# New orders of the matmuls within a head, and the value projection's buffers moved in SBUF

## The chip, the cores and the metric

The kernel runs on one core of a Trainium2 chip. A core has a matrix engine, TensorE (PE in the profile; PEld is its loading of weights), and engines that work beside it: VectorE (DVE), ScalarE (ACT), GpSimd (POOL) and SyncE (SP, used here to issue DMAs). PE writes to PSUM, which has eight banks of 512 fp32 columns; DVE and ACT read from there. The metric is the device time of one execution in microseconds (us), the median of several runs.

## What is computed

Two attentions over the same input x (2048 rows of 576 numbers, 32 heads of 18 numbers each), mixed by a gate:

```python
g = _sigmoid((x * gate_w).sum(-1, keepdims=True))
a = _A_ref(x, A_wqkv, A_wo)      # 32 heads, keys and values of their own
b = _B_ref(x, B_wq, B_wk, B_wv, B_wo)   # 32 heads, one key and value for all
return g * a + (1 - g) * b
```

Each head is `softmax(q @ k.T / sqrt(18)) @ v`. So 64 heads of 2048 x 2048 scores are computed, their exponentials taken, multiplied by the values and normalised, and the two results go through output matrices and are added. The kernel takes the exact maximum of each row of scores before the exponentials.

## The kernel before

**Stages.** First the projections of queries and keys (to DRAM, in two fp16 parts, a high and a low one), then the projection of the values together with the first maxima (T below 0 in the code), then the main stage, and a short last one. Heads u = 0 to 31 are those of B (one key tile, `ksb`), 32 to 63 those of A.

**The main stage** is one loop over T, the tiles of 128 keys: 16 tiles a head, two per step, so eight steps ("rows") a head. Three things run at once at different distances:

- Maxima of the head that comes LEAD = 22 tiles later. A matmul (L537) makes 128 x 512 scores in a bank, DVE takes the maximum of each row (L553). In the strings of the order such a matmul is `m`. `N` is an `m` whose bank and that of the one before are read by one DVE instruction of 1024 columns (L551), when the two banks are neighbours. `x` makes the difference of two key blocks and ACT takes its positive part (L540, tile xb); `c` is the block to which DVE then adds xb while it takes the maximum (L543). So x and c save one reading.
- Scores and exponentials, `s`: a matmul (L598), which ACT reads and exponentiates into one of 16 slots of the tile pt (L587). `S` is an `s` that is read together with the one before in one ACT instruction of 1024 columns, when the two banks are neighbours.
- The product with the values, two tiles later, `p0` and `p1` (L613, four matmuls that fill the columns of the array side by side, each in two passes over fp32): `p0f` is a full tile of 512 columns, `p0h` a half, 256 columns, and a second `h` finishes it. The sums stay in bank 7.

Queries and keys lie twice in SBUF, in rows 0 to 55 for scores and 64 to 117 for maxima, so that a matmul of either kind uses its own half of the array's rows, and two can run side by side.

**Banks.** Scores and x take the least recently used of banks 0 to 3, maxima, c and the output units that of banks 4 to 6. The order of use starts anew with each head.

**The order within a row** is written out by hand as strings, one string a row and eight a head. PE runs them as they stand. There are four sets: PLAIN for heads without output units, ONE for heads with one unit, TWO for two, EACH for the last heads with a unit in every row. A unit `U` is 12 matmuls of the output projection (L742), whose sum goes out by ACT (first part) or DVE (second part). Heads 33 to 52 have units: ONE for 33, 36, 38, 41, 43, 46, 48 and 51, TWO for the other twelve. PLAIN holds for 0 to 32 (but for the first row of head 0, FIRST) and 53 to 58 (but for the last row of 58), EACH from there. `steps_pair` (L920) reads a string and places the operations.

At the end of a head DVE copies bank 7 to the tile oe (L635), in the first row of the next head.

**The value projection's buffers.** `project_v` (L315) writes 32 blocks through three tiles `vst`, by ACT (L321) and then a DMA to v_d, issued from ACT's queue. They are the last tiles of the pool `stp`, on the right side of SBUF. The pools of the first stages (xpool, wpool, stp, later vwp) are laid from the right end inwards; when they are closed (`open_ph2`, L493), pt and others are laid on the left side behind what is there, and the key tiles ksa and others from the right end. Where a new tile lies over an old one, its first write waits for the last use of the old one.

Of the kernel before, what the change touches and what calls it, by code (L numbers as in the profile page):

```python
# [8 lines left out]
F32 = mybir.dt.float32  # L9
# [10 lines left out]
S = 2048  # L20
# [29 lines left out]
def gated_mix_kernel(ctx: ExitStack, tc: tile.TileContext, xT, wall, wv, wo, out):  # L50
    nc = tc.nc
    P = 128
# [80 lines left out]


    ph1 = ExitStack()
    xpool = ph1.enter_context(tc.tile_pool(name="xpool", bufs=1, side="right"))
    wpool = ph1.enter_context(tc.tile_pool(name="wpool", bufs=2, side="right"))
    stp = ph1.enter_context(tc.tile_pool(name="stp", bufs=3, side="right"))
# [169 lines left out]
        nc.vector.tensor_copy(vb[:, 4 * c:4 * c + 4, 0:18],  # L308
                              pv[:, 0:72].rearrange("p (j d) -> p j d", d=18))

    vst = [stp.tile([P, 16, 19], F32, name=f"vst{i}", bufs=1) for i in range(3)]
    for t in vst:
        nc.gpsimd.memset(t, 1.0)

# [550 lines left out]
    def due(T, t0, t1, n):  # L865
        if t0 == SEG[0][3]:
# [6 lines left out]


    FIRST = "s m s c s m s m s m s m s m s x"
    PLAIN = ("c s x s m m S p0h s m s m p0h m s S m s p1f",
# [7 lines left out]
    ONE = ("s m s m p0f m s m s m s p1f s x c s m s U",  # L884
# [7 lines left out]
    TWO = ("p0h s c S m m s p0h p1h m s s m p1h s x s m s m U",  # L892
# [7 lines left out]
    EACH = ("p0f m s s m m s p1f m s s x s c U m s m s",  # L900
# [8 lines left out]
    def pair_order(T):  # L909
        n = len(UNITS.get(T // 16, ()))  # L910
        return (EACH if T >= SEG[1][3] else TWO if n == 2 else ONE if n else PLAIN)[T % 16 // 2]

# [53 lines left out]
    for T in range(-LEAD, NSTEP + 2, 2):  # L966
# [15 lines left out]
        for op in order.split():  # L982
            k, second, c = op[0], op[1:2] == "B", op[2:]
# [86 lines left out]
```

## Time and profile before

| | us |
|---|---|
| Median of 3 runs | 2667.53 (2667.22 to 2669.83) |
| The profiled execution | 2669.34 |
| Its span, first to last instruction | 2667.6 |
| Mean granted clock of PE | 0.996 |
| Projections, up to the first score | 0 to 276.2 |
| Main stage, first to last copy of a finished head | 321.65 to 2610.6 |

The profile is one execution. A row of a timeline has the start, the length, the engine, the line in the code, the operation, the tile written and the tiles read; several instructions of one kind are merged, with their count. What stands in brackets is the idle time before, and what ended it. The length of an instruction on PE, DVE or ACT has a tail in which the next one already runs, so the time that each one costs in a full queue is read from start to start. A windows row has the length of a stretch, the busy time and count of PE, PEld, DVE, ACT and POOL, PE's granted clock (1.00 is full), the share of the DMA engines and GB/s.

### The profile page before, as it was taken

How to read it: one execution, taken by the hardware profiler on the slowest of the kernel's cores; microseconds unless marked ns; L12 is line 12 of the kernel's file. 1: busy time of each engine (PE TensorE's matmuls, PEld its weight loads, DVE VectorE, ACT ScalarE, POOL GpSimd, SP SyncE). 2: the span in 40 equal slices, each digit the busy share in tenths (PEclk: the TensorE clock that was granted, in tenths of full speed). 3: DMA queues.
4: the chain of work that ended last, by engine and by line, in shares of the span. 5: the costliest groups of instructions: out<-in, count | busy, mean ns of one | idle time of the engine just before them, and what ended most of it. 6: DMA issues, size and time to landing. Idle time of an engine off the chain costs nothing.

```text
span 2667.6 us, 59192 instructions
## 1 busy us (share of the span) xinstructions
PE 2643.6 (99%) x22798; PEld 946.5 (35%) x22798; DVE 2406.6 (90%) x4341; ACT 2388.4 (90%) x4334; POOL 284.0 (11%) x526
## 2 busy tenths in 40 slices
PE   9999999999999999999999999999999999999998
PEld 7788322222222222222222323332323332223444
DVE  8447899999999999999999999999999999998873
ACT  4331899999999999999999999999999999998785
POOL 4740000002001100100110001000100021001000
PEclk9999999999999999999999999999999999999999
DMA  6332000011001100110132113112211112123312
GB/s 202 122 114 77 23 20 19 19 31 48 25 20 46 44 19 19 51 36 17 39 77 83 42 47 91 59 34 60 77 52 51 46 59 65 40 60 96 90 36 95
DMA packets 127304, 150.18 MB, mean 56 GB/s; under 512 B 55456, under 2 KB 94744, under 8 KB 125933
## 3 DMA queue, kind: packets, MB, share of 16 engines
q1 hardware_dynamic: 112593, 119.38, 15.8%
q0 software_dynamic: 8096, 19.30, 2.1%
q10 hardware_dynamic: 6332, 7.71, 0.8%
q8 instruction: 179, 2.93, 0.4%
q14 instruction: 104, 0.85, 0.1%
HBM read 90.80 MB, written 46.45 MB: 51 GB/s over the span
## 4 chain that ended last, share of the span: by engine, by line
PE 89%; DVE 6%; ACT 3%; issue 1%; DMA 1%; POOL 0%; SPq 0%; ACTq 0%; DVEq 0%; POOLq 0%
PE bk L613 36%; PE bk L537 20%; PE bk L598 20%; PE bk L267 5%; PE bk L742 4%; DVE mx L553 3%; ACT pt L587 2%; PE bk L318 2%; DVE junk L543 1%; DVE mx L551 1%; DVE norm_a L209 0%; PE bk L807 0%; DVE pl L282 0%; SPq L56 0%; DVE oacc L815 0%
## 5 line engine op out<-in xcount | busy, mean ns | idle before, releaser
L587 ACT ACTIVATE pt<-bk 128x512 f32<-128x512 f32 (+1 forms) x3616 | 2091.4, 667 | 66.3 <-PE bk L598 41.5
L553 DVE TENSOR_REDUCE mx<-bk 128x1 f32<-128x512 f32 x2600 | 1624.5, 682 | 46.7 <-PE bk L537 27.1
L598 PE MATMUL bk<-qs,ksb 56*128 56x512 f16 x2688 | 798.4, 381 | 2.7 <-ACT pt L587 2.5
L537 PE MATMUL bk<-ksb,qs 54*128 54x512 f16 x2363 | 745.2, 381 | 3.5 <-DVE mx L553 1.6
L613 PE MATMUL bk<-pt,vb 128*19 128x256 f32 (+1 forms) x6656 | 593.3, 435 | 0.2 <-PE bk L537 0.2
L613 PE MATMUL bk<-pt,vg 128*19 128x256 f32 (+1 forms) x5504 | 555.1, 480 | 0.0
L537 PEld LDWEIGHTS <-qs 54*128 54x128 f16 x4096 | 290.0, 94 | 547.1 <-issue 478.9
L598 PE MATMUL bk<-qs,ksa 56*128 56x512 f16 x1408 | 404.9, 380 | 1.3 <-ACT pt L587 0.3
L537 PE MATMUL bk<-ksa,qs 54*128 54x512 f16 x1232 | 386.2, 379 | 2.9 <-DVE mx L553 2.2
L543 DVE CUSTOM_DVE_ANT_0 junk<-bk,xb 128x512 bf16<-128x512 f32 x501 | 343.6, 686 | 46.4 <-ACT pt L587 14.9
L598 PEld LDWEIGHTS <-ksb 56*128 56x128 f16 x2688 | 194.5, 94 | 367.2 <-issue 321.5
L540 ACT ACTIVATE xb<-bk 128x512 f32<-128x512 f32 x501 | 304.9, 609 | 5.5 <-PE bk L598 3.9
L551 DVE TENSOR_REDUCE mx<-bk 128x2 f32<-128x1024 f32 x247 | 300.4, 1216 | 1.1 <-PE bk L598 1.0
L613 PEld LDWEIGHTS bk<-pt,vb 128*19 128x19 f32 x6656 | 119.6, 97 | 269.1 <-issue 244.7
L563 POOL TENSOR_SCALAR mt<-mt 128x32 f32<-128x32 f32 x64 | 18.5, 290 | 1624.0 <-DVE mt L561 1624.0
L613 PEld LDWEIGHTS bk<-pt,vg 128*19 128x19 f32 x5504 | 96.8, 97 | 232.2 <-issue 223.8
L598 PEld LDWEIGHTS <-ksa 56*128 56x128 f16 x1408 | 97.1, 94 | 203.7 <-issue 181.5
L537 PE MATMUL bk<-kdb,qs 54*128 54x512 f16 x373 | 141.5, 379 | 0.0
L276 ACT ACTIVATE ph<-bk,tv 128x512 f16<-128x512 f32 x56 | 38.1, 686 | 97.6 <-PE bk L267 61.0
L282 DVE SCALAR_TENSOR_TENSOR pl<-bk,tv,ph 128x512 f16<-128x512 f32 x56 | 41.7, 748 | 71.3 <-ACT ph L276 41.2
L267 PE MATMUL bk<-xh,wh 128*128 128x512 f32 (+1 forms) x295 | 85.9, 389 | 0.8 <-ACT xh L360 0.7
L267 PE MATMUL bk<-xh,wl 128*128 128x512 f32 (+1 forms) x295 | 85.3, 387 | 0.0
(146 smaller groups left out, 1338.2 us busy)
## 6 DMA issues: line engine op xcount, KB each, us to landing
qs<-qkh SPq DMA_DIRECT2D x244, 72.0 KB
qs<-qkl SPq DMA_DIRECT2D x122, 72.0 KB
onh<-oh SPq DMA_DIRECT2D x32, 256.0 KB
onl<-ol SPq DMA_DIRECT2D x32, 256.0 KB
oih<-onh SPq DMA_DIRECT2D x16, 512.0 KB
oil<-onl SPq DMA_DIRECT2D x16, 512.0 KB
ot<-oe SPq DMA_DIRECT2D x220, 36.0 KB
qkh<-ph POOLq DMA_DIRECT2D x56, 128.0 KB, 2.1
```

Of the source, the lines that this page charges most:

```text
L267: nc.tensor.matmul(bk[:, fp, a0:b0], w[a][:kr, k, :], X[b][:kr, k, s0 + a0:s0 + b0], start=(n == 0), stop=(n == len(PROJ) - 1), skip_group ...
L282: nc.vector.scalar_tensor_tensor(l, fp, t, h, op0=OP.mult, op1=OP.subtract)
L318: nc.tensor.matmul(fp[:, 0:288], X[b][:kr, k, st_ * P:(st_ + 1) * P], w[a][:kr, k, :], start=(n == 0), stop=(n == len(PROJ) - 1))
L537: nc.tensor.matmul(pm, qs[u % 3][b:b + 54, i * P:(i + 1) * P], k, start=True, stop=True)
L540: nc.scalar.activation(MX["x", u, i], pm, AF.Relu)
L543: nc.vector.tensor_tensor_reduce(junk, pm, MX.pop(("x", u, i)), 1.0, -3e38, op0=OP.add, op1=OP.max, accum_out=MX[u][:, i, c:c + 1])
L551: nc.vector.tensor_reduce(flat[:, c0:c0 + 2], bk[:, n0:n0 + 2, :], axis=AX.X, op=OP.max)
L553: nc.vector.tensor_reduce(MX[u][:, i, c:c + 1], pm, axis=AX.X, op=OP.max)
L587: nc.scalar.activation(L["pt"][:, t[0]:t[0] + k, :], bk[:, n:n + k, :], AF.Exp, scale=SCALE / LIFT ** 2)
L598: nc.tensor.matmul(bk[:, n, :], kst(u)[b:b + 56, i * P:(i + 1) * P], qs[u % 3][b:b + 56, x * 512:(x + 1) * 512], start=True, stop=True)
L613: nc.tensor.matmul(acc[32 * j:32 * j + 19, a:b], v_of(u, i), PT[u, i, j][:, a:b], start=(i == 0 and a == 0), stop=(i == 15), skip_group_ch ...
L742: nc.tensor.matmul(fp[:, 0:288], o[b][:r, t, s2 * P:(s2 + 1) * P], w[a][:r, t, 288 * hf:288 * hf + 288], start=(n == 0), stop=(n == 3 * nt ...
```

## The change

The three tiles vst get a pool of their own, which is opened first and so lies at the right end of SBUF. The strings of PLAIN, ONE and TWO are replaced; FIRST, EACH and the last head's orders stay. Each row still holds eight s or S, six m or N, one c, one x and the same PV work, and ONE and TWO have their units in the same rows.

```diff
--- before.py
+++ after.py
@@ -133,6 +133,7 @@
 
 
     ph1 = ExitStack()
+    vsp = ph1.enter_context(tc.tile_pool(name="vsp", bufs=1, side="right"))
     xpool = ph1.enter_context(tc.tile_pool(name="xpool", bufs=1, side="right"))
     wpool = ph1.enter_context(tc.tile_pool(name="wpool", bufs=2, side="right"))
     stp = ph1.enter_context(tc.tile_pool(name="stp", bufs=3, side="right"))
@@ -308,7 +309,7 @@
         nc.vector.tensor_copy(vb[:, 4 * c:4 * c + 4, 0:18],
                               pv[:, 0:72].rearrange("p (j d) -> p j d", d=18))
 
-    vst = [stp.tile([P, 16, 19], F32, name=f"vst{i}", bufs=1) for i in range(3)]
+    vst = [vsp.tile([P, 16, 19], F32, name=f"vst{i}") for i in range(3)]
     for t in vst:
         nc.gpsimd.memset(t, 1.0)
 
@@ -873,30 +874,30 @@
 
 
     FIRST = "s m s c s m s m s m s m s m s x"
-    PLAIN = ("c s x s m m S p0h s m s m p0h m s S m s p1f",
-           "s m N s s s m p0f x s c m S p1h m s s m p1h",
-           "m s s c s p0h s m s m x s m p0h p1h m s s m p1h",
-           "s m m s x N s p0h s c p0h m s m s S s m p1f",
-           "s c s x m s m p0h m s m s p0h s m S N s p1h p1h",
-           "x m s m s s m p0f s m m s S s N p1h c s p1h",
-           "m s x s m N S p0h s c p0h s m m s S m s p1f",
-           "s c s m s m p0h m s s x p0h m s S m s m p1f")
-    ONE = ("s m s m p0f m s m s m s p1f s x c s m s U",
-           "m s s c s x p0h s m s m p0h S m m s m S p1f",
-           "s m s m m s p0h s m x s p0h c s S m m s p1f",
-           "m s s c S m s p0h s m p0h m s m x s S m p1f",
-           "c s s m m x s p0h s m m s p0h s m S N s p1f",
-           "m s s N S m s p0f s m m s x N s p1h s c p1h",
-           "s m c s m s p0h s x s m p0h s m S m s m p1f",
-           "s m s m s m s p0f c s s m s m p1f m s x")
-    TWO = ("p0h s c S m m s p0h p1h m s s m p1h s x s m s m U",
-           "s m m s m s p0h m s s x p0h s m s c m s p1f",
-           "s m x m s S m p0h s m p0h s c s m S m s p1f",
-           "m s s m m s p0f s m x s m s m p1f c s s",
-           "m s m s p0f s m s m m s p1f x s s c s m U",
-           "c s m s s m p0h m s s x p0h s m m s S m p1f",
-           "s m s m N s x s m p0f c s m s s m p1f s",
-           "m m s s s m p0f c s m s s N p1h x s m s p1h")
+    PLAIN = ("s m x s c m s p0h m s m s p0h m s s m s p1h p1h",
+           "m s N s c x s p0f s m s S m p1h m s s m p1h",
+           "s m s x m p0h m s s m p0h c s s m S s m p1f",
+           "s m c s m s p0h m s s x p0h m s S m s m p1f",
+           "m s c x s m S p0h s m p0h m s m s S N s p1f",
+           "x s c S m m s p0f m s s m S p1h s m m s p1h",
+           "m s m s p0h m s s x c s p0h s m m S p1h s m p1h",
+           "m s s m S c s p0h m s p0h m s x s m s m p1f")
+    ONE = ("s m s m p0f m s s m m s p1f s x m s s c U",
+           "s m s m S x c p0h m s p0h s m s s m m S p1f",
+           "m s m s N s p0h s m x s p0h s m S c m s p1f",
+           "s m m x s c s p0f s m m s S m s p1h s m p1h",
+           "m s m x s N S p0h s c p0h s m s m S N s p1f",
+           "s m s m s s c p0f x s m m S p1h s m m s p1h",
+           "m s m s p0h m s s x s m p0h s c m S p1h m s p1h",
+           "s m s x c m s p0f m s m s s m p1f m s s")
+    TWO = ("p0f s m m s N S p1h m s p1h s x s m c s U m s",
+           "x m s m S p0h s m p0h s m m s S s c p1h s m p1h",
+           "m s m s s m S p0h s m p0h m s s x m c s p1f",
+           "s m m s c S p0f m s s m s s m p1f s m x",
+           "s m s m p0f s m s c m s p1f x s m s m s U",
+           "m s m s x c s p0f m s m s S s m p1h s m p1h",
+           "m s s m x s c p0f s m s m m s p1f m s S",
+           "s m s c p0f s m m s m s p1f m s m s S x")
     EACH = ("p0f m s s m m s p1f m s s x s c U m s m s",
            "p0f s c s m m S p1f m s s m x s U s m s m",
            "x s U c s S m p0f m s m s s m p1f m S m s",
```

## The prediction

> **What bounds the kernel now.** I read the page first: the busy line says which engines could be the bound, the chain of waits says which one ends last.
>
> ```profile
> span 2667.6 us, 59192 instructions
> PE 2643.6 (99%) x22798; PEld 946.5 (35%) x22798; DVE 2406.6 (90%) x4341; ACT 2388.4 (90%) x4334; POOL 284.0 (11%) x526
> PE 89%; DVE 6%; ACT 3%; issue 1%; DMA 1%; POOL 0%; SPq 0%; ACTq 0%; DVEq 0%; POOLq 0%
> ```
>
> The chain is 89% PE. But the busy line averages over stages, so next the windows view, over one plain head (busy us of PE, PEld, DVE, ACT, POOL after the length):
>
> ```profile
> 640.95:676.39 35.44, 35.44 (x340) 10.08 (x337) 34.78 (x63) 35.41 (x64) 2.58 (x5) 1.00 0.11 34
> ```
>
> Three engines look full, so busy time does not decide; intervals from start to start do. First PE, in the timeline (start, length):
>
> ```profile
> 641.39 0.38 PE L598 MATMUL bk<-qs,ksb 56*128 56x512 f16 x1
> ...
> 641.61 0.38 PE L598 MATMUL bk<-qs,ksb 56*128 56x512 f16 x1
> 641.93 1.05 PE L613 MATMUL bk<-pt,vb 128*19 128x512 f32 x8
> 642.92 0.39 PE L537 MATMUL bk<-kdb,qs 54*128 54x512 f16 x1
> ...
> 643.36 0.38 PE L537 MATMUL bk<-ksb,qs 54*128 54x512 f16 x1
> 643.67 0.63 PE L613 MATMUL bk<-pt,vb 128*19 128x256 f32 x8
> 644.23 0.39 PE L537 MATMUL bk<-ksb,qs 54*128 54x512 f16 x1
> ```
>
> A score (s) and a maximum matmul (m, c, x) sit in different row halves and share a **slot**; slots follow each other in 0.22 us (641.39 to 641.61). From the last slot of a block to the PV piece: 0.31 (643.36 to 643.67). From a half piece (h) to the next block 0.56, from a full one (f) 0.99 (641.93 to 642.92). A second half directly behind another is taken at 0.43, the difference of 0.99 and 0.56.
>
> **Count of a plain head.** A block of a scores and b maxima needs max(a, b) slots. The old PLAIN has 71 slots in 24 blocks, 18 leading halves, 2 adjoining ones and 6 full: 47 x 0.22 + 24 x 0.31 + 18 x 0.56 + 2 x 0.43 + 6 x 0.99 = 34.66 us. The head takes 35.44. So PE has no time to spare but **0.78 us of stalls**, and DVE and ACT, in the same stage:
>
> ```profile
> 641.80 1.21 DVE L551 TENSOR_REDUCE mx<-bk 128x2 f32<-128x1024 f32 x1
> 642.93 0.68 DVE L553 TENSOR_REDUCE mx<-bk 128x1 f32<-128x512 f32 x1
> 639.41 1.87 DVE L553 TENSOR_REDUCE mx<-bk 128x1 f32<-128x512 f32 x3
> 648.66 1.63 ACT L587 ACTIVATE pt<-bk 128x512 f32<-128x512 f32 x3
> L587 ACT ACTIVATE pt<-bk 128x512 f32<-128x512 f32 x3136 | 1674.5, 611 | 50.5 <-PE bk L598 31.0 <-PE bk L537 11.5 <-DMA v_d<-vst 2.7
> L587 ACT ACTIVATE pt<-bk 128x1024 f32<-128x1024 f32 x480 | 496.1, 1035 | 15.8 <-PE bk L598 10.5 <-PE bk L537 4.6
> L551 DVE TENSOR_REDUCE mx<-bk 128x2 f32<-128x1024 f32 x247 | 300.4, 1216 | 1.1 <-PE bk L598 1.0
> ```
>
> One maximum costs DVE 0.60 ((1.87 - 0.68) / 2), a joined pair 1.13 (641.80 to 642.93): a join saves 0.07. For ACT I take 0.48 for one exponential (1.63 less the mean 0.61, halved, is 0.51, with a little waiting in it) and 0.90 for a pair (1.035 less the overlap 0.13): a join saves 0.06. A plain head then asks 34.0 us of ACT and 34.2 of DVE (38 x 0.60, 5 x 1.13, 8 x 0.61, 0.9 for the head's copy and maxima). PE's 34.66 is the largest, the other two are 2% below: stalls come where PE asks for a bank faster than ACT or DVE can hand it back.
>
> **The change, part 1: the orders.** What they change by count:
>
> PLAIN (38.8 heads' worth: 0 to 32, 53 to 57 and most of 58, less head 0's first pair): 70 slots, 25 blocks, 19 leading halves, 1 adjoining, 6 full: 45 x 0.22 + 25 x 0.31 + 19 x 0.56 + 0.43 + 6 x 0.99 = 34.66. Nothing gained. Joined exponentials 9 as before; joined maxima 5 to 2, +0.2 us of DVE per head.
>
> ONE (8 heads) and TWO (12 heads) carry output units. What one unit costs, and what the head groups take (copies of finished heads on DVE):
>
> ```profile
> 1532.47 0.37 PE L598 MATMUL bk<-qs,ksa 56*128 56x512 f16 x1
> ...
> 1532.79 0.79 PE L742 MATMUL bk<-woh,oih 128*128 128x288 f32 x4
> ...
> 1534.58 0.39 PE L598 MATMUL bk<-qs,ksa 56*128 56x512 f16 x1
> ```
>
> ```profile
> 321.65 0.68 DVE L635 COPY oe<-bk 128x512 f32<-128x512 f32 x1
> 1457.72 0.68 DVE L635 COPY oe<-bk 128x512 f32<-128x512 f32 x1
> 2215.37 0.68 DVE L635 COPY oe<-bk 128x512 f32<-128x512 f32 x1
> ```
>
> A unit adds 1534.58 - 1532.47 - 0.22 = 1.89. Counts with units: ONE 35.44 to 35.88 (slots 68 to 69, blocks 22 to 23, halves 12 to 14, full 10 to 9), TWO 36.66 to 37.32 (slots 67 to 69, full 10 to 11, the adjoining halves gone). The mean of the twenty goes from 36.17 to 36.74: **+0.57 us**. They take (2215.37 - 1457.72) / 20 = 37.88, so their stalls are 1.71. TWO's joined exponentials rise from 4 to 8, its joined maxima fall from 2 to 1.
>
> So by PE's count the new orders gain nothing; all they can gain is stalls. To see where stalls must arise I set, for each run of operations on one set of banks, PE's count against what the other engine needs. Reuse times:
>
> ```profile
> 276.18 0.39 PE L537 MATMUL bk<-ksb,qs 54*128 54x512 f16 x1
> ...
> 276.63 0.69 DVE L553 TENSOR_REDUCE mx<-bk 128x1 f32<-128x512 f32 x1 [0.35 <-PE bk L537]
> 277.38 0.37 PE L537 MATMUL bk<-ksb,qs 54*128 54x512 f16 x1
> ```
>
> From a maximum's matmul to DVE's read 0.45 (taken for ACT too), from the read's start to the next matmul in that bank 0.75. For ACT that last step is 0.64 (279.41 to 280.05, rows in part 2). Scores and x share four banks, the maxima three. A run of n reads of scores therefore needs 0.45 + (n - 1) x 0.48 + 0.64 before the fourth operation behind its last one. Example, third row of the old PLAIN, `s s c s p0h s m s m x s`: the first and the seventh score-bank operation lie 2 x 0.22 + 0.31 + 0.56 + 2 x 0.22 = 1.75 us apart by PE's count; three reads need 0.45 + 0.96 + 0.64 = 2.05. It must stall 0.30, and it does, between these two:
>
> ```profile
> 646.87 0.38 PE L598 MATMUL bk<-qs,ksb 56*128 56x512 f16 x1
> ...
> 647.41 0.37 PE L598 MATMUL bk<-qs,ksb 56*128 56x512 f16 x1
> ```
>
> 0.54 us instead of 0.22. The worst run of each set, counted in this way (ACT / DVE): PLAIN 0.30 / 0.24 before, 0.17 / 0.24 after; ONE 0.57 / 0.40 to 0.35 / 0.16; TWO 0.89 / 0.39 to 0.41 / 0.17. The old TWO asks ACT for too much right behind a unit (end of its fifth row to the seventh); the new one puts joins there. PLAIN's maxima stay as uneven as they were. I let the stalls shrink as these sums do: a choice, since the worst run is not all runs. PLAIN 0.54 to 0.41: stalls 0.78 to 0.59, **-0.19 x 38.8 = -7.4 us**. ONE and TWO together 1.16 to 0.55: 1.71 to 0.82, +0.57 - 0.89 = -0.32, **x 20 = -6.4 us**. Bounds: no stall goes, 20 x 0.57 = +11.4; three quarters go, -0.59 x 38.8 + 20 x (0.57 - 1.28) = -37. EACH and the ends are as before.
>
> **Part 2: the value buffers.** The first exponential (timeline) and the stage around it (windows, granted clock behind the busy times):
>
> ```profile
> 276.17 0.39 PE L598 MATMUL bk<-qs,ksb 56*128 56x512 f16 x1
> ...
> 276.72 0.33 ACTq L56 DMA_DIRECT2D v_d<-vst  x1
> ...
> 279.41 1.08 ACT L587 ACTIVATE pt<-bk 128x512 f32<-128x512 f32 x2 [2.72 <-DMA v_d<-vst]
> ...
> 280.05 0.58 PE L598 MATMUL bk<-qs,ksb 56*128 56x512 f16 x1 [2.31 <-ACT pt L587]
> ...
> 316.91 0.38 PE L598 MATMUL bk<-qs,ksb 56*128 56x512 f16 x1
> ```
>
> ```profile
> 275.87:279.28 3.41, 1.83 (x11) 0.60 (x11) 2.91 (x6) 0.41 (x1) 0.00 (x0) 1.00 0.18 58
> 279.28:289.52 10.24, 9.23 (x40) 1.71 (x39) 5.01 (x8) 8.10 (x15) 0.00 (x0) 0.50 0.00 0
> 289.52:292.93 3.41, 3.41 (x36) 0.97 (x36) 3.24 (x7) 3.20 (x7) 0.00 (x0) 1.00 0.02 5
> ```
>
> The first write of pt waits 2.7 us for the last value store, which means that pt lies over a vst buffer. PE then stands 2.31 us, and in the next 10.24 us its clock is 0.50. Head 0 takes 316.91 - 276.17 = 40.74 instead of 35.44: 5.3 lost. With vst at the other end, the next thing late is ACT's own issue of that store (276.72 + 0.33 = 277.05), 2.4 earlier than 279.41. In the window from 275.87 PE then has five or so slots more, and I expect the clock to hold. I take **-5.0 us**; if the clock falls all the same, -2.3. The skill's page "TensorE: Matmul & The Clock Gate" ("Why this matters for your kernels") ties the half clock to a window of idle PE and warns of gaps above some 3 us; here the gap is 2.31 and the window had 1.83 us of matmuls, so by the Trainium skill's rule this wait is not the cause and the gain would be the 2.3. The trace speaks for the wait, as nothing else changes there. What now lies over vst is at the right end, the first ksa tile, whose first write is SP's:
>
> ```profile
> 276.27 1.56 SPq L56 DMA_DIRECT2D ksa<-ones_r  x4
> 305.55 0.35 SPq L56 DMA_DIRECT2D m_d<-mh  x1
> ```
>
> These four would wait until about 279; behind them SP has nothing before 305.55, so 26 us of cover hide it.
>
> **Sum.** -7.4 - 6.4 - 5.0 = -18.8 us. The profiled execution took 2669.3 around its span of 2667.6; the median of the runs is 2667.5, and I subtract from that: 2648.7, told as 2649.
>
> **Rivals.**
> 1. *DVE is the bound* (slower). Joined maxima fall from 247 to 118: three per PLAIN head, one per TWO head. Price: 129 x 0.07 = 9.0 by intervals, 129 x (2 x 0.682 - 1.216) = 19 by mean lengths. With the wait gone 2671 to 2684, middle 2677. It decides once DVE's idle time per plain head, 35.44 - 34.78 = 0.66, no longer covers three lost joins (0.21 to 0.44): this speaks against it; DVE's 98% in that row speaks for it. The Trainium skill ("Perfetto Trace Analysis", "Identifying the Most-Contended Engine") trusts the occupancy of Vector and Scalar and not PE's matmul time; by it ACT and DVE bind here and orders that only rearrange PE gain nothing, which is this rival or the third.
> 2. *PE's count in full*, no stall goes: +11.4 - 5.0, 2674. For: PE's chain share and the count. Against: the stall found where the count puts it.
> 3. *Only the wait goes*, the orders are a draw: 2662.5. The mean of both sides; nothing in particular speaks for it.
> 4. *Three quarters of the stalls go*: -37 - 5, 2625.5. For: PLAIN repeats each head in 35.44, so its stalls are a fixed pattern that an order can remove. Against: PLAIN's DVE runs are no better than before.
>
> **Numbers.** Forecast 0.53, rival 1 0.13, rival 2 0.14, rival 3 0.10, rival 4 0.10. 0.2% is 5.3 us, about what a measurement here can tell from no change. Faster: forecast, rival 4 and half of rival 3, 0.68. Same: the other half of 3 and half of 2, 0.12. Slower: rival 1 and half of 2, 0.20. The range leaves out rival 4's far half and rival 1's upper half: 2626 to 2676; the forecast's own range is 2638 to 2658.
>
> **What would show it.** ACT's first pt write no longer waits for v_d, it starts near 277.05 (in the old times), and the clock stays 1.00 up to 290. Exponentials of 1024 rise from 480 to 530, joined maxima fall from 247 to 118. The copies of finished heads in the plain stage lie 35.25 apart instead of 35.44, the twenty heads take 37.6 on the mean. If plain heads grow and DVE shows no idle time, rival 1 was right; if ONE and TWO heads grow by half a microsecond, rival 2. The forecast is wrong if the stalls don't follow the worst runs.

## The result, and the profile after

The changed kernel takes 2646.6 us, the median of 4 runs (2644.6 to 2646.9), against 2668.7 for the kernel before (2667.2 to 2671.2). The ratio is 0.9915, with a 95% interval of 0.9897 to 0.9932: 22 us faster, where 18.8 were forecast. The sum was near; two of its three terms were not, and their errors go opposite ways.

The page of the changed kernel (its lines are one further down in the code: L599 scores, L538 maxima, L614 PV, L588 exponentials, L636 the copies):

```profile
span 2644.6 us, 59215 instructions
PE 2621.3 (99%) x22758; PEld 940.8 (36%) x22758; DVE 2406.6 (91%) x4470; ACT 2368.5 (90%) x4284; POOL 283.0 (11%) x526
PE 91%; DVE 5%; ACT 1%; DMA 1%; issue 1%; SPq 0%; ACTq 0%; POOL 0%; DVEq 0%
```

PE's share of the chain rose by two points; DVE's and ACT's, in which the waits for banks lie, fell by three. The groups, by form:

```profile
L588 ACT ACTIVATE pt<-bk 128x1024 f32<-128x1024 f32 x530 | 551.1, 1040 | 14.7 <-PE bk L599 12.0 <-PE bk L538 2.8
L552 DVE TENSOR_REDUCE mx<-bk 128x2 f32<-128x1024 f32 x118 | 143.5, 1216 | 0.5 <-PE bk L538 0.4
```

530 joined exponentials and 118 joined maxima, as counted. Where the time went, from the copies of finished heads (timeline of DVE: start, length). Copy 1 closes head 0, copy 33 closes head 32, copy 53 closes head 52:

```profile
318.97 0.68 DVE L636 COPY oe<-bk 128x512 f32<-128x512 f32 x1
...
635.30 0.68 DVE L636 COPY oe<-bk 128x512 f32<-128x512 f32 x1
670.38 0.68 DVE L636 COPY oe<-bk 128x512 f32<-128x512 f32 x1
...
1443.27 0.68 DVE L636 COPY oe<-bk 128x512 f32<-128x512 f32 x1
2194.38 0.68 DVE L636 COPY oe<-bk 128x512 f32<-128x512 f32 x1
```

The table holds the two profiled executions, whose spans differ by 23.0 us:

| Stretch | before, us | after, us | difference | forecast |
|---|---|---|---|---|
| up to the first copy | 321.65 | 318.97 | -2.7 | -5.0 |
| 32 plain heads, to copy 33 | 1136.1 | 1124.3 | -11.8 | -6.1 |
| 20 heads with units, to copy 53 | 757.7 | 751.1 | -6.5 | -6.4 |
| the rest, to the span's end (plain heads 53 to 58 in it) | 452.2 | 450.2 | -2.0 | -1.3 |

A plain head takes 35.07 us (635.30 to 670.38, rounded) instead of 35.44. Every seventh takes longer, about 35.8 us instead of about 36.0. In the windows view of that head all three engines still look full, and DVE now leaves 0.24 us idle instead of 0.66:

```profile
635.30:670.37 35.07, 35.07 (x338) 9.86 (x336) 34.83 (x66) 35.06 (x64) 2.57 (x5) 1.00 0.11 34
```

The first row of the main stage, by timeline and windows (granted clock behind the five busy times):

```profile
276.23 0.39 PE L599 MATMUL bk<-qs,ksb 56*128 56x512 f16 x1
...
277.45 4.03 ACT L588 ACTIVATE pt<-bk 128x512 f32<-128x512 f32 x8 [0.71 <-PE bk L599]
...
278.10 0.37 PE L599 MATMUL bk<-qs,ksb 56*128 56x512 f16 x1 [0.30 <-ACT pt L588]
...
278.90 1.58 SPq L56 DMA_DIRECT2D ksa<-ones_r  x4
```

```profile
276.23:280.30 4.07, 3.44 (x18) 1.07 (x18) 3.73 (x9) 3.26 (x7) 0.00 (x0) 1.00 0.12 40
280.30:287.13 6.83, 6.78 (x31) 1.17 (x30) 3.89 (x7) 5.25 (x10) 0.00 (x0) 0.50 0.02 5
```

The wait for v_d is gone: ACT starts at 277.45 and not at 279.41. SP's four issues wait for the value store now, 278.90 instead of 276.27, and nobody waits for them. But the clock still falls, at 280.30, and stays at half for 6.83 us.

### The profile page after: what moved, and what is told of

Its sections match the earlier page's. It is cut to its first block, busy times and chain, and to the rows that moved or that the text cites. A ratio compares the mean times of both kernels' runs of the same rounds, so it can differ in the third digit from the quotient of the medians.

```text
span 2644.6 us, 59215 instructions
## 1 busy us (share of the span) xinstructions
PE 2621.3 (99%) x22758; PEld 940.8 (36%) x22758; DVE 2406.6 (91%) x4470; ACT 2368.5 (90%) x4284; POOL 283.0 (11%) x526
## 4 chain that ended last, share of the span: by engine, by line
PE 91%; DVE 5%; ACT 1%; DMA 1%; issue 1%; SPq 0%; ACTq 0%; POOL 0%; DVEq 0%
PE bk L614 38%; PE bk L538 24%; PE bk L599 17%; PE bk L268 5%; PE bk L743 4%; DVE mx L554 3%; PE bk L319 2%; ACT pt L588 1%; DMA wst<-wall 1%; DVE norm_a L210 0%; DVE junk L544 0%; SPq L56 0%; DVE oacc L816 0%; DVE pl L283 0%; PE bk L626 0%
## 5 line engine op out<-in xcount | busy, mean ns | idle before, releaser
L588 ACT ACTIVATE pt<-bk 128x512 f32<-128x512 f32 (+1 forms) x3566 | 2078.0, 686 | 65.9 <-PE bk L599 45.5
L554 DVE TENSOR_REDUCE mx<-bk 128x1 f32<-128x512 f32 x2858 | 1785.9, 683 | 69.0 <-PE bk L538 38.4
L599 PE MATMUL bk<-qs,ksb 56*128 56x512 f16 x2688 | 798.8, 380 | 1.4 <-ACT pt L588 0.9
L538 PE MATMUL bk<-ksb,qs 54*128 54x512 f16 x2363 | 737.3, 381 | 1.5 <-DVE mx L554 1.3
L614 PE MATMUL bk<-pt,vb 128*19 128x256 f32 (+1 forms) x6656 | 599.5, 435 | 0.1
L614 PE MATMUL bk<-pt,vg 128*19 128x256 f32 (+1 forms) x5464 | 558.8, 482 | 0.0
L538 PEld LDWEIGHTS <-qs 54*128 54x128 f16 x4096 | 290.2, 94 | 613.0 <-issue 530.9
L599 PE MATMUL bk<-qs,ksa 56*128 56x512 f16 x1408 | 403.8, 380 | 3.0 <-ACT pt L588 2.0
L538 PE MATMUL bk<-ksa,qs 54*128 54x512 f16 x1232 | 388.1, 380 | 2.4 <-DVE mx L554 2.1
L599 PEld LDWEIGHTS <-ksb 56*128 56x128 f16 x2688 | 199.8, 93 | 298.8 <-issue 255.3
L614 PEld LDWEIGHTS bk<-pt,vb 128*19 128x19 f32 x6656 | 116.3, 97 | 276.1 <-issue 255.7
L614 PEld LDWEIGHTS bk<-pt,vg 128*19 128x19 f32 x5464 | 93.8, 97 | 219.0 <-issue 214.8
L599 PEld LDWEIGHTS <-ksa 56*128 56x128 f16 x1408 | 100.1, 93 | 191.8 <-issue 158.6
L552 DVE TENSOR_REDUCE mx<-bk 128x2 f32<-128x1024 f32 x118 | 143.5, 1216 | 0.5 <-PE bk L538 0.4
L538 PE MATMUL bk<-kdb,qs 54*128 54x512 f16 x373 | 141.1, 378 | 0.1
```

The source lines that it names most:

```text
L538: nc.tensor.matmul(pm, qs[u % 3][b:b + 54, i * P:(i + 1) * P], k, start=True, stop=True)
L552: nc.vector.tensor_reduce(flat[:, c0:c0 + 2], bk[:, n0:n0 + 2, :], axis=AX.X, op=OP.max)
L554: nc.vector.tensor_reduce(MX[u][:, i, c:c + 1], pm, axis=AX.X, op=OP.max)
L588: nc.scalar.activation(L["pt"][:, t[0]:t[0] + k, :], bk[:, n:n + k, :], AF.Exp, scale=SCALE / LIFT ** 2)
L599: nc.tensor.matmul(bk[:, n, :], kst(u)[b:b + 56, i * P:(i + 1) * P], qs[u % 3][b:b + 56, x * 512:(x + 1) * 512], start=True, stop=True)
L614: nc.tensor.matmul(acc[32 * j:32 * j + 19, a:b], v_of(u, i), PT[u, i, j][:, a:b], start=(i == 0 and a == 0), stop=(i == 15), skip_group_ch ...
```

## The experiments

First each part of the change alone, and the cause of the half clock.

**Buffers alone.** The changed kernel with the old strings of PLAIN, ONE and TWO:

```diff
+    vsp = ph1.enter_context(tc.tile_pool(name="vsp", bufs=1, side="right"))
...
-    vst = [stp.tile([P, 16, 19], F32, name=f"vst{i}", bufs=1) for i in range(3)]
+    vst = [vsp.tile([P, 16, 19], F32, name=f"vst{i}") for i in range(3)]
```

> The value buffers moved, all orders as before. Theory (the move is worth only its wait, since the clock still falls at the next window's end): the first write of pt no longer waits for v_d, first score to first copy of a finished head shrinks from 45.48 us by 2.0 to 2.6, the granted clock still shows 0.50 for some windows near 280 to 290, and all later stages keep their lengths (321.65 to 1457.72 = 1136.1, to 2215.37 = 757.7). Rival (the whole 2.7 us that the changed kernel gains there is the move, or 5 with a steady clock): 2.7 or more, later stages the same.

Ratio to the kernel before 0.9989 (0.9980 to 0.9998). Its rows, the first score and the copies 1, 33 and 53:

```profile
275.96 0.39 PE L599 MATMUL bk<-qs,ksb 56*128 56x512 f16 x1
...
318.57 0.68 DVE L636 COPY oe<-bk 128x512 f32<-128x512 f32 x1
...
1455.11 0.68 DVE L636 COPY oe<-bk 128x512 f32<-128x512 f32 x1
2212.33 0.68 DVE L636 COPY oe<-bk 128x512 f32<-128x512 f32 x1
```

```profile
282.20:285.60 3.40, 3.21 (x13) 0.47 (x13) 0.87 (x2) 2.06 (x4) 0.00 (x0) 0.50 0.00 0
```

From the first score to the first copy 42.61, 2.9 less than 45.48. That passes the expected 2.6, and by its number the rival holds: the move alone brings all that the changed kernel gains in this stretch. The clock fell here too, but for 3.4 us only. Later stages keep their lengths (1136.5, 757.2).

How long the clock stays at half is not fixed by the kernel. Two of the kernels tried further on have the buffers and the first row of the changed one, and differ from it only in joins of PLAIN; one shows 3.41 us at half (no joined maxima, first two rows), the other 6.82 (no joined exponentials):

```profile
280.42:283.83 3.41, 3.35 (x14) 0.47 (x13) 1.01 (x4) 2.19 (x5) 0.00 (x0) 0.50 0.00 0
283.83:287.25 3.42, 3.42 (x38) 0.84 (x37) 3.27 (x6) 3.34 (x7) 0.00 (x0) 1.00 0.00 0
279.35:286.17 6.82, 6.76 (x31) 1.19 (x32) 4.09 (x7) 5.41 (x11) 0.00 (x0) 0.50 0.02 5
```

So a difference of a few tenths in this stretch, from one trace a kernel, is not told from chance. Over all kernels tried, one trace each, the move itself is clear:

| Kernels | stretch at half clock, us | first score to first copy, us |
|---|---|---|
| buffers in the old place, 8 | 6.8 in four, 10.2 in four | 44.30 to 45.48 |
| buffers moved, 5 | 3.4 in three, 6.8 in two | 42.03 to 42.83 |

**PLAIN alone**, and **ONE and TWO alone**: the kernel before with only these strings replaced by those of the diff.

> New PLAIN alone, ONE, TWO and the buffers as before. Theory (each set works by itself): the 32 plain heads take 1124.3 us as in the changed kernel instead of 1136.1, the twenty heads with units stay at 757.7; in all about -14 us with heads 53 to 58. Rival (the sets gain by what the heads next to them hand over): the twenty heads move too, by over 1 us.

> New ONE and TWO, PLAIN and the buffers as before. Theory: the twenty heads take 751.1 us as in the changed kernel instead of 757.7, plain heads 35.44 as before; in all -6 to -7 us. Most of it in the eight ONE heads (37.1 to 36.5 on the mean), little in the twelve TWO heads (38.4 to 38.25). Rival (the new ONE and TWO gain only after the new PLAIN): the twenty heads gain under 4 us.

PLAIN alone: 0.9937 (0.9920 to 0.9953), medians 16.6 us apart where about 14 were expected. ONE and TWO alone: 0.9979 (0.9969 to 0.9989), 4.9 us where 6 to 7 were expected. The stages themselves came as expected, but for the twenty heads with PLAIN alone. Their copies 1, 33 and 53, PLAIN alone first:

```profile
319.84 0.68 DVE L635 COPY oe<-bk 128x512 f32<-128x512 f32 x1
1444.40 0.68 DVE L635 COPY oe<-bk 128x512 f32<-128x512 f32 x1
2200.68 0.68 DVE L635 COPY oe<-bk 128x512 f32<-128x512 f32 x1
```

```profile
320.10 0.68 DVE L635 COPY oe<-bk 128x512 f32<-128x512 f32 x1
1456.34 0.68 DVE L635 COPY oe<-bk 128x512 f32<-128x512 f32 x1
2207.70 0.68 DVE L635 COPY oe<-bk 128x512 f32<-128x512 f32 x1
```

PLAIN alone gives plain heads of 1124.6 in all and leaves the twenty at 756.3 (1.4 under before, past the rival's 1 us). The same strings of ONE and TWO take anything from 756.4 to 758.5 in the other kernels here that keep them, so these 1.4 us say little. ONE and TWO alone give 751.4 for the twenty and leave the plain heads at 1136.2. So each set works by itself, as far as one trace a kernel can tell.

**The clock.** Five more matmuls in PE's gaps of the first row, on a tile of zeros; `d` is their sign in the string:

```diff
+    fill = fixed.tile([P, 512], F16, name="fill")
...
+    nc.gpsimd.memset(fill, 0.0)
...
-    FIRST = "s m s c s m s m s m s m s m s x"
+    FIRST = "s m s c s m s m d s m d s m d s m d s x d"
...
+            elif op == "d":
+                nc.tensor.matmul(acc, fill[SB:SB + 56, 0:P], fill[SB:SB + 56, :], start=True, stop=True,
+                                 skip_group_check=True)
```

> The changed kernel with five more matmuls of 56 rows and 512 columns on zeros in the first row of head 0, in PE's gaps there; they write bank 7, which the first PV piece overwrites, so nothing that is read changes. Theory (the clock falls because PE has too little work in the window before 280): the granted clock stays 1.00 from 276 to 290 and the first score to first copy shrinks from 42.74 to 39.5 to 40.5 us. Rival (the fall has another cause, or these matmuls count for too little): the clock shows 0.50 all the same and the stretch is as long or up to 1 us longer.

Median 2645.1 us, ratio to the kernel before 0.9909 (0.9895 to 0.9924). The windows view over its first row and the 10 us behind, which begins with the first score, and the first copy:

```profile
276.78:290.02 13.24, 12.23 (x98) 3.43 (x101) 11.61 (x21) 12.29 (x25) 0.00 (x0) 1.00 0.05 16
```

```profile
317.48 0.68 DVE L638 COPY oe<-bk 128x512 f32<-128x512 f32 x1
```

The clock holds at 1.00 and the stretch takes 40.70 instead of 42.74: 2.0 us, a little less than expected (39.5 to 40.5). All 13 traces without the filling show a stretch at half clock here, the one with it shows none. So the fall comes from too little work on PE, and no longer from the wait, as far as one trace with the filling can show it. By the trace this version is 2.0 us faster in this stretch than the changed kernel; the intervals of the two ratios overlap, so the times alone don't tell the two apart.

Then the size of PLAIN's gain, twice what was forecast. First the joins:

```diff
-           "s m N s s s m p0f x s c m S p1h m s s m p1h",
+           "s m m s s s m p0f x s c m S p1h m s s m p1h",
...
```

that is, N read as m in all rows of the old PLAIN, and the same in the new one.

> The kernel before with each joined maximum of PLAIN (N) read singly (m), five a head. Theory A (the new PLAIN gains 0.38 us a head because a join keeps two of three banks for 1.13 us, and it has three fewer): a plain head falls from 35.44 us to 35.3 or less. Theory B (it gains by where the scores stand, so by ACT's runs): the head does not fall; with 0.35 us more of DVE it stays within 0.1 or rises.

> The changed kernel with PLAIN's last two joined maxima read singly too. Theory A: a plain head falls below 35.07 us. Theory B: it stays within 0.05 or rises by up to 0.15, the price of 0.13 us more of DVE.

From copy to copy, old without joined maxima 35.51, new without 35.16:

```profile
606.46 0.68 DVE L635 COPY oe<-bk 128x512 f32<-128x512 f32 x1
641.97 0.68 DVE L635 COPY oe<-bk 128x512 f32<-128x512 f32 x1
```

```profile
634.14 0.68 DVE L636 COPY oe<-bk 128x512 f32<-128x512 f32 x1
669.30 0.68 DVE L636 COPY oe<-bk 128x512 f32<-128x512 f32 x1
```

Both heads get longer, by 0.07 and 0.09. Fewer joins are not what helps, and theory A falls.

**One row.** The row whose stall the prediction showed:

```diff
-           "m s s c s p0h s m s m x s m p0h p1h m s s m p1h",
+           "s m s x m p0h m s s m p0h c s s m S s m p1f",
```

> The kernel before with only the third row of PLAIN taken from the new one (the row with the worst run of scores, short by 0.30 us, of which the trace showed 0.32 between two score matmuls). Theory of the worst run: a plain head falls by 0.1 to 0.3 us from 35.44. Rival (a stall taken away here comes up in a later row, since DVE and ACT are 98% and more in use): it falls by less than 0.05 or not at all.

```profile
603.74 0.68 DVE L635 COPY oe<-bk 128x512 f32<-128x512 f32 x1
639.23 0.68 DVE L635 COPY oe<-bk 128x512 f32<-128x512 f32 x1
```

35.49: slightly longer, with PE's count the same. The theory of the worst run falls here.

**No joined exponentials** in the new PLAIN (S read as s):

> The changed kernel with PLAIN's nine joined exponentials read singly: 0.5 us more of ACT a head, 34.5 in all. Theory B (ACT's runs set PLAIN's stalls): a plain head rises from 35.07 by 0.2 us or more. Rival (maxima and DVE set them): it rises by less than 0.1.

```profile
636.64 0.68 DVE L636 COPY oe<-bk 128x512 f32<-128x512 f32 x1
671.94 0.68 DVE L636 COPY oe<-bk 128x512 f32<-128x512 f32 x1
```

35.30: 0.23 more, for about 0.5 us more of ACT. ACT counts, at about half its price.

**Halves of the head.** Four rows new, four rows old, and the other way round; a PV piece ends each half, so no block of matmuls runs across.

> The kernel before with the first four rows of PLAIN new, the last four old. PE's count of this head is 34.44 us (34.66 for old and new). Theory of rows (a stall belongs to its own rows; by row, old rows 0 to 3 take 17.74 us and new ones 17.56): a plain head takes 35.25 to 35.30. Theory of the count (the head follows PE's count, stalls unchanged): 35.22 or less, and 0.44 less than with the other half new. Rival (stalls move along the head): 35.4 or more.

> The same with the last four rows new, the first four old. PE's count 34.88 us. Theory of rows (old rows 4 to 7 take 17.70 us, new ones 17.51): 35.23 to 35.28. Theory of the count: 35.66. Rival (stalls move along the head): 35.4 to 35.5.

First half new, 35.25; second half new, 35.26:

```profile
639.71 0.68 DVE L635 COPY oe<-bk 128x512 f32<-128x512 f32 x1
674.96 0.68 DVE L635 COPY oe<-bk 128x512 f32<-128x512 f32 x1
```

```profile
602.89 0.68 DVE L635 COPY oe<-bk 128x512 f32<-128x512 f32 x1
638.15 0.68 DVE L635 COPY oe<-bk 128x512 f32<-128x512 f32 x1
```

Each half gains 0.18 to 0.19 and the two add up to the whole. PE's count differs by 0.44 between these two kernels, their heads do not: the count theory falls.

**One more cut** of a PV piece in the new PLAIN:

```diff
-           "s m c s m s p0h m s s x p0h m s S m s m p1f",
+           "s m c s m s p0h m s s x p0h m s S m p1h s m p1h",
```

> The changed kernel with the last full PV piece of PLAIN's fourth row cut in two halves with a slot between them: 0.22 us more of PE's count a head, ACT and DVE the same. Theory of the count: a plain head rises from 35.07 by 0.15 to 0.25 us. Rival (PE waits for ACT and DVE anyhow): it rises by less than 0.08.

```profile
633.88 0.68 DVE L636 COPY oe<-bk 128x512 f32<-128x512 f32 x1
669.08 0.68 DVE L636 COPY oe<-bk 128x512 f32<-128x512 f32 x1
```

35.20, or 0.13 more for 0.22 us more of PE: between the two.

**Two rows.** The second and third rows new, the rest old:

> The kernel before with the second and third rows of PLAIN new. The third alone had made the head 0.05 us longer, rows 0 to 3 together 0.19 shorter. Theory of neighbours (a row's stall hangs on what the row before it leaves to DVE and ACT, so the second row brings the third's gain): a plain head takes 35.32 to 35.40 instead of 35.44, its third row about 4.42 instead of 4.49. Rival (the gain needs all four rows): 35.44 or more, the third row 4.5 or more.

```profile
637.81 0.68 DVE L635 COPY oe<-bk 128x512 f32<-128x512 f32 x1
673.15 0.68 DVE L635 COPY oe<-bk 128x512 f32<-128x512 f32 x1
```

35.34, so the second row brings the gain that the third alone had not. The third row has the same string in both kernels; here is its last block, `c s s m S s m`, up to the PV piece, with the old second row ahead of it and with the new one:

```profile
645.91 0.39 PE L537 MATMUL bk<-ksb,qs 54*128 54x512 f16 x1
...
646.65 0.68 DVE L543 CUSTOM_DVE_ANT_0 junk<-bk,xb 128x512 bf16<-128x512 f32 x1
...
647.09 1.05 PE L613 MATMUL bk<-pt,vb 128*19 128x512 f32 x8
```

```profile
644.34 0.39 PE L537 MATMUL bk<-ksb,qs 54*128 54x512 f16 x1
...
644.93 0.68 DVE L543 CUSTOM_DVE_ANT_0 junk<-bk,xb 128x512 bf16<-128x512 f32 x1
...
645.37 1.05 PE L613 MATMUL bk<-pt,vb 128*19 128x512 f32 x8
```

1.18 us against 1.03, where PE's count asks for 0.97. The whole third row takes 4.57 and 4.42 us, the latter as expected, and this is all that the two heads differ by. DVE begins to read `c` 0.74 us after the block's start with the old second row ahead and 0.59 with the new one, while ACT begins on the row's `x` 1.39 and 1.40 us after the row's start. So what a row stalls hangs on the row before it, and what that row hands on here is a DVE that is 0.15 us late.

## Why the prediction was right or wrong

**The sum and the direction** were right: 2649 forecast, 2646.6 measured. That the sum came so near is partly luck. The plain heads gained twice what was forecast (11.8 for 6.1 us over 32 of them), the buffers about half (2.7 for 5.0).

**The orders gain stalls and nothing else.** By PE's count old and new PLAIN are equal at 34.66, and the head fell by 0.37; ONE and TWO went up by 0.57 in the count and fell by 0.33. That step stands. But the count is no floor under the head that stalls are simply added to: the two half-new heads differ by 0.44 in the count and by 0.01 in time, and one more cut of 0.22 cost 0.13.

**The size of PLAIN's term failed**: -0.19 a head was forecast, -0.37 came. Of the 0.78 us of stalls about half went, between the quarter of the forecast and the three quarters of rival 4. The step that failed is "I let the stalls shrink as these sums do". The worst run is no measure of a head's stalls. With the third row new, PLAIN's worst run of scores is gone and the head is not shorter: the stall comes up again in the last block of the same row, where DVE is late. Only with its neighbour does the row gain (35.34), and each half of the head gains its own share. The prediction named that risk ("the worst run is not all runs") and still took the ratio.

That the twenty heads came out at -6.5 against -6.4 is luck. Taken for each set by itself, the same ratio gives -0.35 for a ONE head and -0.29 for a TWO head. The copies show -0.59 (37.10 to 36.51 on the mean) and -0.15 (38.40 to 38.26). The two errors cancel in the mean.

**What decides a plain head**: no single engine. In the new head, added DVE work of 0.13 us cost 0.09, added ACT work of 0.5 cost 0.23, added PE work of 0.22 cost 0.13. Each costs between 0.4 and 0.7 of its length, which fits that PE, ACT and DVE take turns. Rival 1 (DVE the bound) is out by the measured time; that DVE is nearly full is true, though, with 0.24 us left a head.

**Where the stalls lay.** The groups of DVE in the plain heads from 322 to 1443 us show it: `c`, the read that needs ACT's xb, with the idle time of DVE just before it behind the last bar. In order: the kernel before, the changed one, first half new, second half new.

```profile
L543 DVE CUSTOM_DVE_ANT_0 junk<-bk,xb 128x512 bf16<-128x512 f32 x252 | 172.6, 685 | 15.8 <-ACT pt L587 10.9
L544 DVE CUSTOM_DVE_ANT_0 junk<-bk,xb 128x512 bf16<-128x512 f32 x254 | 173.3, 682 | 0.0
L543 DVE CUSTOM_DVE_ANT_0 junk<-bk,xb 128x512 bf16<-128x512 f32 x254 | 173.4, 683 | 8.1 <-ACT pt L587 5.0 <-PE bk L537 0.2
L543 DVE CUSTOM_DVE_ANT_0 junk<-bk,xb 128x512 bf16<-128x512 f32 x254 | 174.0, 685 | 7.5 <-PE bk L598 5.4
```

With the old strings DVE stood 15.8 us in front of `c`, most of it put down to ACT, and nowhere else in its maxima. With the new ones it stands 0.0 us there and 3.5 us before its other maxima. Each half removes about half of this wait; the third row alone, which gained nothing, leaves it at 16.3. The difference, 12.3 us, is about what the 32 heads gained, 11.8 us. The prediction's sums set PE against the readers of a bank and have no term for DVE's wait for xb. That this wait is what held PE was not tested: no run moves `x` and `c` alone, so the cause of the size stays open there.

**The buffers' term was too large**: -5.0 forecast, -2.7 came (with the orders' share of head 0 in it; the buffers alone, -2.9). The step that failed is "I expect the clock to hold". The wait went, as read, and 2.0 us with it at the first exponential (277.45 for 279.41; I had 277.05, the end of ACT's issue, and 0.35 us lie between that issue's end and the exponential). The clock fell all the same, at 280.30 instead of 279.28. The prediction's other end, -2.3 "if the clock falls all the same", was the nearer one. The Trainium skill ("TensorE: Matmul & The Clock Gate", "Why this matters for your kernels") ties the fall to a window of idle PE; by that rule the wait of 2.31 us was not the cause, and the prediction worked out the -2.3 from it. The trace bears that out for the wait but not for the idle time: the clock fell in the changed kernel with no gap of PE over 0.30 us since the first score.

**SP's issues** for ksa waited 2.6 us and were hidden, as costed.

## What to carry to other kernels

When three engines are each within 2% of the largest (34.66, 34.2 and 34.0 us here), count each one's start-to-start work first, then judge an order by whole neighbouring rows: a row can keep its stall because the row before it leaves an engine late. Don't size a gain by the worst stall, and look also at reads that need another engine's result. Where a stage begins with a stretch limited by another engine, look at the granted clock behind it: here the price of a short wait, or of thin work, was the half-rate stretch that followed. And check a forecast term by term, since a near sum can hide errors that cancel.

## What the hardware showed that was not expected

In the changed kernel the granted clock fell to 0.50 although PE had stood for no more than 0.3 us before a matmul: from 276.23 to 280.30 the records show PE busy for 3.44 of 4.07 us with 18 matmuls of 54 or 56 rows. Five more such matmuls on zeros kept it at 1.00 in the one trace that has them. PE's busy time does not decide it: the last 3.41 us before the fall show 2.79 us busy and 13 matmuls, and in the filled kernel 2.74 us busy with 17 matmuls (280.51 to 283.92) went by without a fall. How much work is enough was not measured. The half-rate stretch was 10.24 us in the kernel before, 6.83 in the changed one and about 3.4 with the buffers alone, one to three times the same length, and it varies between kernels with the same first row.

Most plain heads of the changed kernel repeat to within 0.02 us (all but every seventh), and the same row's string takes 0.15 us more or less by what stood ahead of it.
